# An exponential on VectorE in half octaves: two factors in place of a cubic, in a kernel that shares softmax between ScalarE and VectorE

## The chip, the cores and the metric

The kernel runs on one core of a Trainium2 chip. The metric is device time in microseconds: 894.55 us for the kernel before, the median of three runs (894.08 to 895.09). The profile is of one further execution with a span of 894.9 us. PE is TensorE, DVE VectorE, ACT ScalarE, POOL GpSimd, SP the engine that issues the DMAs.

## What is computed

Two identical layers of a transformer, one after the other, on 2048 tokens of width 448, in bf16:

```python
x = x + A(layernorm(x))     # attention: 16 heads of 28
x = x + B(layernorm(x))     # dense 448 -> 1792 -> 448, squared relu
x = x + A(layernorm(x))
x = x + B(layernorm(x))

# A:  q, k, v = x @ wqkv ; scores = q k^T / sqrt(28)
#     p = softmax(scores) ; o = p @ v ; o @ wo
# B:  h = x @ w1 + b1 ; r = max(h, 0) ; (r * r) @ w2 + b2
```

There is no mask. Each layer has 16 x 2048 x 2048 scores, and each of them goes through an exponential. Nothing is subtracted ahead of it; the sum of the exponentials comes out of the same matmul as the values (a column of ones beside each head's values), and one reciprocal at the end divides.

## The kernel before

**Units and groups.** Attention is cut in units: one head, 128 x 4 keys for one query block of 128, or 128 x 2 keys for a query block of 256, so 512 columns of scores on 128 partitions, one bank of PSUM. `s_stream` (from line 745) takes three units at a time into one score tile of three banks, of which there are two. The matmuls of line 809 fill it. Then line 834, in `e_stream`, exponentiates the tile on ScalarE in one instruction into a bf16 tile `pt`: 1536 columns for three units. Line 982 in `p_stream` multiplies the exponentials with the values into `oT`.

**Units on VectorE.** Where the function `apart` (line 703) allows it, the third bank of a tile holds a unit that ScalarE does not take. ScalarE then exponentiates 1024 columns, and VectorE does the third bank in its own way. The score tile is free for the next matmuls when both have read it (`o.need = 2`, line 789). `apart` looks at what VectorE has been given over the last `SPAN` us of planned time (at most `BUSY`, or `LOW` where the dense layers are behind schedule), at free buffers and at dependencies.

**The exponential on VectorE** (`a_unit` and `a_rest`, lines 880 to 926). The query weights are scaled so that a score is a power of two times 2^FRAC. Line 892 adds a bias, takes a floor and writes the score as int32, so its upper 16 bits are a whole exponent n and its lower 16 bits a fraction f. Line 909 works out a polynomial in f by Horner's rule, in three instructions of the form (h + b) * f. Line 904 writes n times 128 plus a constant as int16, which read as bf16 is 2^n. Line 915 closes: (h + b0) * 2^n, in bf16, into a buffer `pd`. `set_of` (line 869) gives a unit one of two pairs of stores, `v_i` and `v_h` or a part of the key tile that is not in use, and a store `v_e` each for the powers. So one unit is six VectorE instructions.

**What sets the order.** The program's order on every engine is worked out ahead by a list scheduler, the class `Planner`, in Python when the kernel is built. Each piece of work is an `Op` with an engine, a duration that the writer estimated, dependencies and buffers to acquire. A stream is a generator of `Op`s with a priority; the planner takes the candidate that could start first, and by priority among equals. Nothing is reordered at run time. So a changed estimate moves instructions on every engine. The rest of a VectorE unit has a priority that falls as it gets old (the `V_` constants, line 898). Other streams carry the layernorms, the projections and the dense layers (`chain`, from line 1116, with the rectifier of line 1160 and the square of line 1167), the division (`norm_pair`, `norm_stream`), and two that keep TensorE occupied: the score matmuls are written again up to three times (`again`, line 800), and `heat` (line 1203) adds matmuls on a scratch bank.

Of the kernel before, what the change touches and what calls it, by code (L numbers as in the profile page):

```python
# [11 lines left out]
DT = mybir.dt  # L12
AF = mybir.ActivationFunctionType
ALU = mybir.AluOpType
P = 128
# [7 lines left out]

FRAC = 16
EXP_BIAS = -0.207249953 * 2.0 ** FRAC
EXP_LOW = -56.0 * 2.0 ** FRAC
EXP_FIELD = 57.0
EXP_POLY = (73.8872584799254, 51.2040206965149, 17.83949703532682, 3.842974297166197)  # L30
OVER = 0.08
COLD = 7.0
WQD = 1
# [2 lines left out]
DCLK = 0.2  # L36
OWN = 2
HALF = 320
LINES = ((280, 1312, 7.8), (1440, 2040, 7.0))
MARGIN = 2.0  # L40
LOW = 0.6
TURNS = 1
# [13 lines left out]
V_PRIO = 6.0  # L56
V_LATE = 3.6
V_LAST = 1.8
V_AGE = 6
V_PAST = 2  # L60
OWN3 = 0
FIRST = 90
V_FIRST = 9.2
V_WAIT = 5.0
NEAR = 9
FAR = 15
KEEP = 4
# [1 line left out]
LEAD = 20  # L69
LAST = 690  # L70
BUSY = 0.95
SPAN = 12.0
NPT = 11
NOS = 3
AEND = 8
# [142 lines left out]
def kernel(  # L218
# [12 lines left out]
    nc = tc.nc  # L231
# [7 lines left out]

    q_scale = float(DH) ** -0.5 * float(np.log2(np.e)) * 2.0 ** FRAC  # L240

# [5 lines left out]
    const = ctx.enter_context(tc.tile_pool(name="const", bufs=1))  # L247
# [13 lines left out]
    pl = Planner()  # L261
# [164 lines left out]
    e_now = [0, 0]  # L426
# [249 lines left out]
    ends_at = {pi: i for i, (pi, *_) in enumerate(units)}  # L676
# [4 lines left out]
    at = [0]  # L681
# [6 lines left out]
    def behind(i):  # L688

        l = 0 if i < LINES[0][1] else 1  # L690
        a, b, n = LINES[l]
        return done[l] < (min(i, b) - a) / (b - a) * n * per[l] - MARGIN
    pending = [0]

    def sets_of(unit):

        pi, kb, r, hh = unit
        l, qb, *_ = passes[pi]
        if l == 0:
            return R_v if 2 <= qb <= 6 else R_v[:1]  # L700
        return R_v

    def apart(i, now, us, soon=SOON):
# [20 lines left out]
        if any(pl.tok.get(d) is None or pl.tok[d].end + LAT["DVE"] > now for d in needs(units[j])):  # L724
            return None
        if pl.load(SPAN, "DVE") > (LOW if behind(i) else BUSY):
            return None
# [17 lines left out]
    def s_stream():  # L745
        while at[0] < len(units):
# [5 lines left out]
            def fn(e, gi=gi, us=us, js=js):  # L752
# [17 lines left out]
                if j is None:  # L770
                    next_at(js[-1] + 1)
                else:
                    if not own:
                        us, ks = us[:2], ks[:2]
                        gbuf[gi]["n"] = 2
                    us, ks = us + [units[j]], ks + [3]
                    taken.add(j)
                    held[0] += 1
                    pending[0] += 1
                    next_at(at[0])  # L780
                    if own:
                        x = gbuf[gi]["x"] = Op("PE", 0.0, None)
                        x.res = min((r for r in R_m if r.when() is not None), key=lambda r: r.when())
                        x.turn = len(x.res.rel)
                        x.res.rel.append(None)
                        dst.append(bank(x, "mt"))
                    else:
                        x = gbuf[gi]["x"] = o
                        o.need = 2
                    pl.spawn(C_PRIO, a_unit(gi, x, dst[-1], us[-1], passes[us[0][0]][0]))  # L790
# [28 lines left out]
    def apart_from(gi, t):  # L819

        if "read" in gbuf[gi]:
            tc.declare_no_dep(t.ins, gbuf[gi]["read"].ins, reason="both read the scores, in banks of their own")
        gbuf[gi]["read"] = t

    def e_stream():
        gi = 0
        while gi < len(gbuf) or s_left:
# [3 lines left out]
            def fn(e, gi=gi, n=n):  # L831
                e_now[:] = [e_now[0] + n // 512 + ("x" in gbuf[gi]), gi]
                pt = gbuf[gi]["pt"] = ptp.tile([P, 3 * 512], DT.bfloat16, name="pt")
                t = nc.scalar.activation(out=pt[:, 0:n], in_=gbuf[gi]["sc"][:, 0:n], func=AF.Exp,  # L834
                                         scale=float(np.log(2.0)) * 2.0 ** -FRAC)
                if gbuf[gi].get("x") is gbuf[gi]["s"]:
# [8 lines left out]
    def pd_free(unit):  # L845

        pi, kb, r, hh = unit
        l, qb, *_ = passes[pi]
        if l == 0:
            return (R_pd[0], *(R_pd[1:5] if qb <= 6 else R_pd[3:5]))  # L850
        if len(norm_done.get((0, len(blocks[0]) - 1), ())) < G:
            return tuple(R_pd[:1])
        return tuple(R_pd[:1] + R_pd[6:]) if hidden_left[0] else tuple(R_pd[:1] + R_pd[5:])

    def pd_of(o):
        i = R_pd.index(o.res)
        if i == 0:
            return vp.tile([P, 512], DT.bfloat16, name="pd")[:, :]
        if i < 5:
            return V_sb[1][:, 11 + i, :, :].rearrange("p h r -> p (h r)")  # L860
        if i > 5:
            return V_sb[0][:, 8 + i, :, :].rearrange("p h r -> p (h r)")
        return hp.tile([P, QB], DT.bfloat16, name="h")[:, :]

    v_i = const.tile([P, 512], DT.int32, name="v_i")
    v_h = const.tile([P, 512], DT.float32, name="v_h")
    v_e = [const.tile([P, 512], DT.int16, name=f"v_e{i}") for i in range(2)]

    def set_of(res, l):

        k = R_v.index(res)
        two = lambda a: a.rearrange("p (a n) -> p a n", a=2)
        if k == 0:
            i, h = two(v_i[:, :]), two(v_h[:, :])
        else:
            keys = K_sb[1 - l][:, :, S - 512:S] if l == 0 else K_sb[0][:, :, 0:512]
            i, h = keys[:, 0:2, :].bitcast(DT.int32), keys[:, 2:4, :].bitcast(DT.float32)
        return i, h, two(v_e[k][:, :]), two

    def a_unit(gi, x, src, unit, l):  # L880
        yield Op("-", 0.0, None, deps=[("s", gi)])
        b0, b1, b2, b3 = [b * 2.0 ** (FRAC * (4 - k)) for k, b in enumerate(EXP_POLY)]
        box = {}

        def take(e):
            pending[0] -= 1
            box["i"], box["h"], box["e"], two = set_of(c.res, l)
            box["two"] = two
            halves = box["i"].bitcast(DT.uint16).rearrange("p a (n t) -> p a n t", t=2)
            box["f"] = halves[:, :, :, 0]  # L890
            box["n"] = box["i"].bitcast(DT.int16).rearrange("p a (n t) -> p a n t", t=2)[:, :, :, 1]
            t = nc.vector.tensor_scalar(out=box["i"], in0=two(src), scalar1=EXP_BIAS,  # L892
                                        scalar2=EXP_LOW, op0=ALU.add, op1=ALU.max)
            if x is gbuf[gi]["s"]:
                apart_from(gi, t)
        c = Op("DVE", 0.69, take, deps=[("s", gi)], acq=sets_of(unit), rel=x)
        yield c
        pl.spawn(lambda now: V_LAST if e_now[1] - gi >= V_AGE or at[0] > ends_at[unit[0]] + V_PAST else V_LATE if now > c.end + V_WAIT else V_PRIO if gi > FIRST else V_FIRST, a_rest(gi, c, box, unit, (b0, b1, b2, b3)))

    def a_rest(gi, c, box, unit, bs):  # L900
        b0, b1, b2, b3 = bs

        def power(e):
            nc.vector.tensor_scalar(out=box["e"], in0=box["n"], scalar1=128.0, scalar2=128.0 * EXP_FIELD,  # L904
                                    op0=ALU.mult, op1=ALU.add)

        def step(b, begin=False):
            def fn(e):
                nc.vector.scalar_tensor_tensor(out=box["h"], in0=box["f"] if begin else box["h"], scalar=b,  # L909
                                               in1=box["f"], op0=ALU.add, op1=ALU.mult)  # L910
            return fn

        def close(e):
            pd = gbuf[gi]["pd"] = pd_of(o)
            nc.vector.scalar_tensor_tensor(out=box["two"](pd), in0=box["h"], scalar=b0,  # L915
                                           in1=box["e"].bitcast(DT.bfloat16), op0=ALU.add, op1=ALU.mult)
        h = Op("DVE", 0.68, step(b3, True), deps=[c])
        yield h
        p = Op("DVE", 0.42, power, deps=[c])
        yield p  # L920
        for b in (b2, b1):
            h = Op("DVE", 0.68, step(b), deps=[h])
            yield h
        o = Op("DVE", 0.68, close, deps=[h, p], acq=lambda: pd_free(unit), rel=c, sets=("x", gi))
        gbuf[gi]["x"] = o
        yield o

# [341 lines left out]
```

The softmax here doesn't subtract the row's maximum and nothing guards it: scores larger than these inputs give would overflow.

## Time and profile before

| Engine | busy us | share of the span | instructions |
|---|---|---|---|
| TensorE, matmuls | 832.2 | 93% | 12829 |
| VectorE | 794.1 | 89% | 1572 |
| ScalarE | 879.0 | 98% | 707 |
| GpSimd | 38.9 | 4% | 98 |

| Instructions | engine | count | busy us |
|---|---|---|---|
| exponentials, line 834 | ScalarE | 683 (555 of 1536 columns, 128 of 1024) | 864.2 |
| VectorE units: line 892 | VectorE | 127 | 86.9 |
| line 909 | VectorE | 381 | 260.2 |
| line 904 | VectorE | 127 | 53.1 |
| line 915 | VectorE | 127 | 86.6 |
| score matmuls, line 809 | TensorE | 5848 | 325.6 |

The busy time of a group is the sum of what its instructions took; where instructions overlap on their engine, groups add up to more than the engine's own busy time. A share of the span is a mean over stages, so the prediction goes through the stretches of the span and the waits before it names a bound. One of the 128 short groups of ScalarE is the last of all, which has two units only; the other 127 have a unit on VectorE.

### The profile page before, as it was taken

Reading aid. Unit: us, or ns where it says so; the run is one execution under the profiler, and the core shown is the slowest. Engines: PE = TensorE matmul, PEld = TensorE weight load, DVE = VectorE, ACT = ScalarE, POOL = GpSimd, SP = SyncE. Lnnn points to the kernel's source line nnn. Section 1 sums busy time; section 2 is a strip of 40 time slices with the busy share of each in tenths; the row PEclk is TensorE's granted clock in tenths of the full one; section 3 lists DMA queues with packets and bytes.
Section 4 is the critical chain, followed back from the end, with each engine's and each line's share of the span. In section 5 each row is a group of like instructions: output and inputs, shape, how many; then the busy total and the mean of one; then the engine's idle time right before and its main releaser. Section 6 shows DMA issues by size and latency. Waiting matters only on the chain.

```text
span 894.9 us, 29098 instructions
## 1 busy us (share of the span) xinstructions
PE 832.2 (93%) x12829; PEld 458.9 (51%) x12829; DVE 794.1 (89%) x1572; ACT 879.0 (98%) x707; POOL 38.9 (4%) x98
## 2 busy tenths in 40 slices
PE   8999999999999999999989998888999999999998
PEld 4555654554545545454554554444544544545566
DVE  7988999999889999999989999889898999989654
ACT  8999999999999999999999999999999999999995
POOL 3100000000000000100000000001000000000000
PEclk9999999999999999999999999999999999999999
DMA  9100100000000000000000000011000000000100
GB/s 263 37 3 3 27 20 10 14 14 15 14 2 15 14 15 14 13 10 8 2 1 3 2 2 2 3 39 37 13 17 19 20 25 19 20 8 19 32 13 18
DMA packets 33915, 18.43 MB, mean 21 GB/s; under 512 B 18874, under 2 KB 33339, under 8 KB 33788
## 3 DMA queue, kind: packets, MB, share of 16 engines
q1 hardware_dynamic: 33788, 16.58, 6.6%
q8 instruction: 100, 1.64, 0.8%
q14 instruction: 27, 0.22, 0.1%
HBM read 14.26 MB, written 2.07 MB: 18 GB/s over the span
## 4 chain that ended last, share of the span: by engine, by line
ACT 69%; issue 12%; PE 9%; DVE 6%; DMA 2%; SPq 1%; POOL 0%; DVEq 0%; ACTq 0%
ACT pt L834 69%; PE sc L809 3%; PE mt L553 3%; PE oT L982 2%; DVE v_h L909 1%; DMA dn<-oT_sb 1%; DVE K_sb L909 1%; DMA rec<-scr 1%; DVE r L1160 1%; PE sc L553 1%; DVE st L448 1%; DVE oTn L1104 0%; SPq L303 0%; DMA x_sb<-in_A_x_dram 0%; DVE v_e L904 0%
## 5 line engine op out<-in xcount | busy, mean ns | idle before, releaser
L834 ACT ACTIVATE pt<-sc 128x1536 bf16<-128x1536 f32 (+1 forms) x683 | 864.2, 1568 | 3.4 <-PE sc L809 3.1
L809 PE MATMUL sc<-Q_sb,K_sb 32*128 32x256 bf16 (+1 forms) x5848 | 325.6, 266 | 53.5 <-ACT pt L834 47.9
L809 PEld LDWEIGHTS <-K_sb 32*128 32x128 bf16 x5848 | 157.9, 92 | 229.9 <-issue 201.1
L982 PE MATMUL oT<-pt,V_sb 128*32 128x256 bf16 (+1 forms) x4094 | 152.7, 269 | 0.6 <-DVE xnT L505 0.3
L553 PE MATMUL mt<-xnT,w 128*128 128x256 bf16 (+1 forms) x928 | 120.6, 269 | 1.0 <-DVE r L1160 0.7
L982 PEld LDWEIGHTS <-V_sb 128*32 128x32 bf16 x4352 | 92.0, 96 | 47.8 <-issue 44.5
L909 DVE SCALAR_TENSOR_TENSOR K_sb<-K_sb 128x512 f32<-128x512 uint16 x165 | 112.9, 684 | 0.9 <-PE mt L553 0.2
L909 DVE SCALAR_TENSOR_TENSOR v_h<-v_h,v_i 128x512 f32<-128x512 f32 x144 | 98.2, 682 | 0.6
L553 PEld LDWEIGHTS <-w 128*128 128x128 bf16 x952 | 78.5, 98 | 35.7 <-issue 27.4
L1160 DVE TENSOR_SCALAR r<-mt 128x512 bf16<-128x512 f32 x106 | 72.2, 681 | 14.8 <-PE mt L553 14.5
L553 PE MATMUL mt<-w,V_sb 128*128 128x448 bf16 (+2 forms) x288 | 67.6, 345 | 0.0
L892 DVE TENSOR_SCALAR v_i<-sc 128x512 int32<-128x512 f32 x72 | 49.3, 685 | 9.7 <-PE sc L809 9.3
L1113 DVE TENSOR_TENSOR x_sb<-x_sb,mt 128x448 bf16<-128x448 bf16 (+2 forms) x63 | 37.8, 604 | 13.4 <-PE mt L553 13.4
L909 DVE SCALAR_TENSOR_TENSOR v_h<-v_i 128x512 f32<-128x512 uint16 x72 | 49.1, 682 | 0.5
L470 POOL TENSOR_TENSOR ve<-mv,eps_t 128x2 f32<-128x2 f32 (+1 forms) x34 | 8.8, 258 | 842.2 <-DVE mv L449 842.2
L1218 PE MATMUL mt<-xn,ident 128*128 128x448 bf16 x130 | 43.5, 357 | 0.5 <-DVE x_sb L1113 0.3
L892 DVE TENSOR_SCALAR K_sb<-sc 128x512 int32<-128x512 f32 x55 | 37.6, 684 | 5.7 <-PE sc L809 5.5
L448 DVE BATCH_NORM_STATS2 st<-x_sb 128x6 f32<-128x448 bf16 x64 | 39.3, 615 | 1.2 <-DMA x_sb<-in_A_x_dram 1.0
L553 PEld LDWEIGHTS <-V_sb 128*128 128x128 bf16 x302 | 24.8, 98 | 25.5 <-issue 11.2
L915 DVE SCALAR_TENSOR_TENSOR V_sb<-v_h,v_e 128x512 bf16<-128x512 f32 x46 | 31.4, 682 | 0.3
L1167 DVE TENSOR_TENSOR V_sb<-r 128x512 bf16<-128x512 bf16 (+1 forms) x69 | 28.7, 417 | 2.1 <-ACT r L1158 1.5
L904 DVE TENSOR_SCALAR v_e<-v_i 128x512 int16<-128x512 int16 x72 | 30.1, 418 | 0.0
(106 smaller groups left out, 733.6 us busy)
## 6 DMA issues: line engine op xcount, KB each, us to landing
rec<-scr SPq DMA_DIRECT2D x56, 128.0 KB
x_sb<-in_A_x_dram SPq DMA_DIRECT2D x8, 224.0 KB
out_dram<-x_sb SPq DMA_DIRECT2D x15, 112.0 KB
w<-in_B_w_dram SPq DMA_DIRECT2D x1, 1568.0 KB
w<-in_B_w_dram SPq DMA_DIRECT2D x1, 1344.0 KB
dn<-oT_sb SPq DMA_DIRECT2D x56, 4.0 KB
V_sb<-in_A_wqkv_dram SPq DMA_DIRECT2D x4, 168.0 KB
scr<-dn SPq DMA_DIRECT2D x28, 8.0 KB
```

Of the source, the lines that this page charges most:

```text
L448: nc.vector.bn_stats(out=st[:, :], in_=x_sb[:, t0 + j, :])
L553: nc.tensor.matmul(box["t"][:, c0:c0 + n], lhsT=lhsT() if callable(lhsT) else lhsT, rhs=rhs, start=a, stop=b)
L809: nc.tensor.matmul(dst[k][:, i * nt * P:(i + 1) * nt * P], lhsT=K_sb[l][rows, g, (kb + i) * P:(kb + i + 1) * P], rhs=Q_sb[rows, g, t0 * P: ...
L834: t = nc.scalar.activation(out=pt[:, 0:n], in_=gbuf[gi]["sc"][:, 0:n], func=AF.Exp, scale=float(np.log(2.0)) * 2.0 ** -FRAC)
L892: t = nc.vector.tensor_scalar(out=box["i"], in0=two(src), scalar1=EXP_BIAS, scalar2=EXP_LOW, op0=ALU.add, op1=ALU.max)
L904: nc.vector.tensor_scalar(out=box["e"], in0=box["n"], scalar1=128.0, scalar2=128.0 * EXP_FIELD, op0=ALU.mult, op1=ALU.add)
L909: nc.vector.scalar_tensor_tensor(out=box["h"], in0=box["f"] if begin else box["h"], scalar=b, in1=box["f"], op0=ALU.add, op1=ALU.mult)
L915: nc.vector.scalar_tensor_tensor(out=box["two"](pd), in0=box["h"], scalar=b0, in1=box["e"].bitcast(DT.bfloat16), op0=ALU.add, op1=ALU.mult)
L982: nc.tensor.matmul(box["t"][DHP * hh:DHP * hh + DHP, 0:n], lhsT=V_sb[l][:, kb + i, 4 * g + hh, :], rhs=p[:, c0:c0 + n], start=begin and kb ...
L1113: nc.vector.tensor_tensor(out=x_sb[:, tb, lo:hi], in0=x_sb[:, tb, lo:hi], in1=t[:, 0:hi - lo], op=ALU.add)
L1160: nc.vector.tensor_scalar(out=r[:, 0:w], in0=t[:, 0:w], scalar1=0.0, scalar2=None, op0=ALU.max)
L1218: nc.tensor.matmul(t[:, 0:D], lhsT=ident[:, :], rhs=xns[0][:, 0:D], start=True, stop=True)
```

## The change

The exponential on VectorE gets another form. The integer is now in half octaves: `FRAC` is 17, so the upper 16 bits of the int32 count halves of a power of two, and the lower 16 bits are the fraction of a half octave. A float whose bits are n times 2^22 plus a constant has mantissas that take two values in turn, half a unit apart. With an offset of 13573 x 2^7, which is 0.2071 of the mantissa's range, they are 1.2071 and 1.7071, whose ratio is the square root of two, as is that of 2.4142 to 1.7071; so bits that are linear in n give exact half octaves. The new line 904 writes these bits as int32 into `v_e`, a store of 32-bit elements now, and they are read as fp32. A third-degree polynomial in the fraction is split in two factors: the linear one multiplies the power (`first`), the quadratic one is worked out as (f + lin) * f (`square`) and closed with a constant in the last instruction. So one unit is five instructions: line 890 (as 892), 904 (power), 910 (`first`), 916 (`square`), 923 (`close`). In the power's place in the planner the estimate stays at 0.42 us; the chain of estimates loses one of 0.68 us.

Around it, four constants of the planner are changed: the target for the dense layers' progress in the first layer (`LINES`), two that set when a unit's rest gets urgent (`V_AGE`, `V_WAIT`), and the window over which VectorE's load is judged (`SPAN`).

```diff
-FRAC = 16
-EXP_BIAS = -0.207249953 * 2.0 ** FRAC
+FRAC = 17
+EXP_BIAS = -0.19498194355419685 * 2.0 ** FRAC
 EXP_LOW = -56.0 * 2.0 ** FRAC
-EXP_FIELD = 57.0
-EXP_POLY = (73.8872584799254, 51.2040206965149, 17.83949703532682, 3.842974297166197)
+EXP_BASE = 72.0 * 2.0 ** 23 + 13573.0 * 2.0 ** 7
+EXP_POLY = (4.12317870205982 * 2.0 ** 16, 3.06764719893404 * 2.0 ** 16, 29.439149859494734 * 2.0 ** 32)
-LINES = ((280, 1312, 7.8), (1440, 2040, 7.0))
+LINES = ((280, 1312, 8.0), (1440, 2040, 7.0))
-V_AGE = 6
+V_AGE = 7
-V_WAIT = 5.0
+V_WAIT = 4.5
-SPAN = 12.0
+SPAN = 14.0
...
-    v_h = const.tile([P, 512], DT.float32, name="v_h")
-    v_e = [const.tile([P, 512], DT.int16, name=f"v_e{i}") for i in range(2)]
+    v_e = const.tile([P, 512], DT.int32, name="v_e")
...
-            nc.vector.tensor_scalar(out=box["e"], in0=box["n"], scalar1=128.0, scalar2=128.0 * EXP_FIELD,
+            nc.vector.tensor_scalar(out=box["e"], in0=box["n"], scalar1=2.0 ** 22, scalar2=EXP_BASE,
                                     op0=ALU.mult, op1=ALU.add)
-
-        def step(b, begin=False):
-            def fn(e):
-                nc.vector.scalar_tensor_tensor(out=box["h"], in0=box["f"] if begin else box["h"], scalar=b,
-                                               in1=box["f"], op0=ALU.add, op1=ALU.mult)
-            return fn
+        p = Op("DVE", 0.42, power, deps=[c])
+        yield p
+
+        def first(e):
+            nc.vector.scalar_tensor_tensor(out=flt("e"), in0=box["f"], scalar=root, in1=flt("e"),
+                                           op0=ALU.add, op1=ALU.mult)
+        g = Op("DVE", 0.68, first, deps=[p])
+        yield g
+
+        def square(e):
+            nc.vector.scalar_tensor_tensor(out=flt("i"), in0=box["f"], scalar=lin, in1=box["f"],
+                                           op0=ALU.add, op1=ALU.mult)
+        h = Op("DVE", 0.68, square, deps=[c])
+        yield h
 
         def close(e):
             pd = gbuf[gi]["pd"] = pd_of(o)
-            nc.vector.scalar_tensor_tensor(out=box["two"](pd), in0=box["h"], scalar=b0,
-                                           in1=box["e"].bitcast(DT.bfloat16), op0=ALU.add, op1=ALU.mult)
-        h = Op("DVE", 0.68, step(b3, True), deps=[c])
-        yield h
-        p = Op("DVE", 0.42, power, deps=[c])
-        yield p
-        for b in (b2, b1):
-            h = Op("DVE", 0.68, step(b), deps=[h])
-            yield h
-        o = Op("DVE", 0.68, close, deps=[h, p], acq=lambda: pd_free(unit), rel=c, sets=("x", gi))
+            nc.vector.scalar_tensor_tensor(out=box["two"](pd), in0=flt("i"), scalar=low, in1=flt("e"),
+                                           op0=ALU.add, op1=ALU.mult)
+        o = Op("DVE", 0.68, close, deps=[g, h], acq=lambda: pd_free(unit), rel=c, sets=("x", gi))
```

## The prediction

> **What bounds the kernel now.** I read the page's busy times first, then its chain, then the groups with shapes kept apart, then stretches of the span, and last the waits of the three busy engines. Busy shares alone leave three candidates:
>
> ```profile
> PE 832.2 (93%) x12829; PEld 458.9 (51%) x12829; DVE 794.1 (89%) x1572; ACT 879.0 (98%) x707; POOL 38.9 (4%) x98
> ```
>
> The chain names one of them:
>
> ```profile
> ACT 69%; issue 12%; PE 9%; DVE 6%; DMA 2%; SPq 1%; POOL 0%; DVEq 0%; ACTq 0%
> ACT pt L834 69%; PE sc L809 3%; PE mt L553 3%; PE oT L982 2%; DVE v_h L909 1%; DMA dn<-oT_sb 1%; DVE K_sb L909 1%; DMA rec<-scr 1%; DVE r L1160 1%; PE sc L553 1%; DVE st L448 1%; DVE oTn L1104 0%; SPq L303 0%; DMA x_sb<-in_A_x_dram 0%; DVE v_e L904 0%
> ```
>
> It is ScalarE's exponential, line 834. The stretches (engine busy us, instruction count) say that this holds nearly everywhere:
>
> ```profile
> core 0: us, PE busy (x) PEld busy (x) DVE busy (x) ACT busy (x) POOL busy (x), PEclk, DMA share, GB/s
> 100.00:580.00 480.00, 447.99 (x6747) 242.94 (x6748) 444.93 (x858) 479.00 (x382) 18.70 (x48) 1.00 0.04 10
> 580.00:645.00 65.00, 57.11 (x913) 31.76 (x908) 58.59 (x122) 63.85 (x51) 2.75 (x6) 1.00 0.11 28
> 645.00:800.00 155.00, 146.03 (x2160) 75.73 (x2157) 141.60 (x273) 155.00 (x125) 3.02 (x7) 1.00 0.06 19
> 800.00:878.00 78.00, 73.27 (x1547) 44.87 (x1548) 54.34 (x108) 78.00 (x61) 1.63 (x4) 1.00 0.08 22
> ```
>
> ScalarE is idle for 1 us of 480, 1.2 of 65, none of 233; VectorE is idle for 35, 6 and 37 of the same. The waits (total us, times, longest us) say who is late for whom; for VectorE I show its costliest and the two of line 892, which reads the scores. ScalarE:
>
> ```profile
> ACT pt L834 <- PE sc L809: 3.1, 8, 0.7
> ```
>
> and in the other direction
>
> ```profile
> PE sc L809 <- ACT pt L834: 47.9, 130, 0.9
> ```
>
> and VectorE's own:
>
> ```profile
> DVE r L1160 <- PE mt L553: 14.5, 22, 1.9
> DVE v_i L892 <- PE sc L809: 9.3, 10, 1.9
> DVE K_sb L892 <- PE sc L809: 5.5, 7, 2.1
> ```
>
> TensorE waits 47.9 us for ScalarE to free score banks, ScalarE 3.1 us for TensorE; VectorE, where it waits, waits for TensorE. So the span is paced by ScalarE from 20 us to 878 us, and what counts is how many score units ScalarE has to exponentiate. VectorE's 7% of idle time in the middle (35 of 480) is the reserve that lets it take units over.
>
> **Prices.** Groups with shapes kept apart (count | busy us, mean ns of one):
>
> ```profile
> L834 ACT ACTIVATE pt<-sc 128x1536 bf16<-128x1536 f32 x555 | 776.1, 1647 | 2.8 <-PE sc L809 2.5 <-ACT pt L834 0.2
> L834 ACT ACTIVATE pt<-sc 128x1024 bf16<-128x1024 f32 x128 | 147.9, 1225 | 0.6 <-PE sc L809 0.6
> L909 DVE SCALAR_TENSOR_TENSOR v_h<-v_h,v_i 128x512 f32<-128x512 f32 x144 | 98.2, 682 | 0.6
> L1160 DVE TENSOR_SCALAR r<-mt 128x512 bf16<-128x512 f32 x105 | 71.8, 683 | 14.8 <-PE mt L553 14.5
> L892 DVE TENSOR_SCALAR v_i<-sc 128x512 int32<-128x512 f32 x72 | 49.3, 685 | 9.7 <-PE sc L809 9.3
> L904 DVE TENSOR_SCALAR v_e<-v_i 128x512 int16<-128x512 int16 x72 | 30.1, 418 | 0.0
> ```
>
> The reader should see two things. A two-unit group is 1647 - 1225 = 422 ns shorter than a three-unit one. And a 512-wide VectorE instruction costs 0.68 us, except line 904, which costs 0.42. Durations overlap on the engines, so I use the pace. On ScalarE the 683 groups keep it busy for 864.2 us (page, part 5): 555a + 128b = 864.2 with a - b = 0.422 gives a = 1.344 and b = 0.922 us. On VectorE the timeline gives starts:
>
> ```profile
> 310.56 0.69 DVE L892 TENSOR_SCALAR v_i<-sc 128x512 int32<-128x512 f32 x1 [1.63 <-PE sc L809]
> 311.28 0.69 DVE L909 SCALAR_TENSOR_TENSOR v_h<-v_i 128x512 f32<-128x512 uint16 x1
> 311.89 0.68 DVE L892 TENSOR_SCALAR K_sb<-sc 128x512 int32<-128x512 f32 x1
> 312.49 0.42 DVE L904 TENSOR_SCALAR v_e<-v_i 128x512 int16<-128x512 int16 x1
> 312.82 0.69 DVE L909 SCALAR_TENSOR_TENSOR v_h<-v_h,v_i 128x512 f32<-128x512 f32 x1
> ```
>
> A full instruction takes 0.60 us from start to start (311.89 to 312.49), line 904 0.33 us, and an instruction right behind the one whose result it reads 0.12 us more (310.56 to 311.28: 0.72).
>
> **What the Trainium skill says.** "VectorE: DVE Perf Modes", section on the TRN2 errata, gives ScalarE 172 cycles plus one per element at 1.2 GHz for a PSUM source; per 512 elements that is 427 ns, and the trace agrees with 422. The same page, section "The perf-mode tier table", gives `tensor_scalar` twice the rate for fp32 within SBUF (1227 ns for 2048 elements) and a two-tensor operation 1x in fp32; its section "Why PSUM operands drop a tier" leaves 1x to an fp32 PSUM operand. The trace agrees where it has the cases: 0.68 us for the two-tensor line 909 and for lines 892 and 1160, whose source lies in PSUM; 0.42 us for the SBUF-only line 904, although its input has a step of two. No row of before has a 32-bit output at the double rate. "SBUF — State Buffer", section "Who interferes with whom", says that such a double-rate instruction blocks GpSimd while it runs; GpSimd is busy for 38.9 us in all, and line 904 is of that kind already.
>
> **The change part by part.** (1) A unit on VectorE has six instructions before: 892, 909 three times, 904, 915; five after: 890, 904, 910, 916, 923, with one of the cubic's steps gone. Four of the five keep their kind (PSUM to int32; two-tensor with a strided uint16; two-tensor that closes in bf16), so 0.60 us each. (2) The power instruction, new line 904, now writes int32 instead of int16. Between SBUF tiles, with [...] one source, I take the double rate, 0.33 us; the bounds are 0.33 and 0.60 (the row of line 1160). So a unit goes from 5 x 0.60 + 0.33 = 3.33 us to 4 x 0.60 + 0.33 = 2.73, or 3.00 at the dear end. (3) The planner, at 0.68 us less a unit in its own account, gives VectorE more units. The built order of the changed kernel has 150 of them instead of 127, still in 683 ScalarE groups: 532 of three units and 151 of two, instead of 555 and 128. So 23 groups shrink by 0.422 us: 23 x 0.422 = 9.7 us off ScalarE, on the path. (4) VectorE in sum: 127 x 3.33 = 423 us before, 150 x 2.73 = 410 after, 13 less, on an engine that is not the bound. Its other instructions are the same but for one rectifier that moves from ScalarE to it (0.6 us, after the last exponential). (5) TensorE issues 116 fewer score matmuls (5848 to 5732; these are repeats that keep it occupied) and 6 fewer filler matmuls (130 to 124). It has 47.9 us of waiting to give; I cost this at nothing, hidden behind ScalarE. (6) The half-octave constants, the bias and the floor are immediates: nothing. Line 834's scale is one too. The second store v_e goes and v_h becomes v_e; the unit's close (line 923) is still what releases the pair of tiles, and the chain behind it has one step less. (7) The planner's constants (the lines for the dense layers' progress 7.8 to 8.0, ages, the load window of 14 us) cost nothing themselves; they move where units lie. Two-unit groups that follow each other directly go from 30 to 37 times; there are no three in a row.
>
> Sum: 894.55 - 9.7 = 884.9 us, if the opening (to 20 us), the tail (878 to 895 us, whose order is the same but for that rectifier) and the present stalls stay.
>
> No wait is added. The wait that could lengthen is TensorE's for a bank that VectorE must read: the tile of scores is released by ScalarE and by line 890 both, and behind that matmul queue all later scores. With less VectorE work per us it should not.
>
> **Rivals.** *Stalls eat part of it.* ScalarE's path from 9.5 to 879 us holds some jitter and hand-over beyond its pace, and a two-unit group leaves TensorE 0.42 us less to refill. For: more pairs of short groups. Against: 3.1 us of waits now. If each of the 23 new short groups cost a wait of 0.2 us (the mean of the present 8 is 0.4), that is 4.6 us: 889.5.
>
> *VectorE becomes the bound* (the slower side). If the int32 output runs at 1x, VectorE's units cost 150 x 3.00 = 450 us, 27 more than now. From 60 to 800 us it is busy for 681 of 740 us (stretches of 20 to 120 us added up), 59 idle, mostly waiting for TensorE. About nine tenths of the 27, 24 us, fall there: 705 of the 731 us that ScalarE would need. If its waits fell to 26 us nothing would be lost; if they stayed at 59 the stretch would last 764, 33 more. Half way is 17 more: 885 + 17 = 902, slower. For: no row of before shows this form. Against: the price in the skill, and line 904's rate despite its strided read.
>
> *TensorE becomes the bound and the time stays.* It is busy for 93%, but a busy matmul engine is not one at its peak, as the skill's opening page "Trainium Kernel Development and Optimization" (section "Performance Expectations") warns too, and it waits 47.9 us for ScalarE here. It would have to lose all that: 894.5.
>
> **How the numbers follow.** Clean gain, 882 to 888 us: 0.65. Part eaten, 888 to 892.8: 0.20. No change, within 0.2% (892.8 to 896.3): 0.05. VectorE-bound or otherwise slower, around 902: 0.10. The likeliest gives 884.9. The range takes the first two cases with a little for a better hand-over than now, 881.5 to 893; the 0.33 us bound lies in it, the dear 0.60 us bound mostly beyond it, which is in the 2 in 10 left out.
>
> **What would show it.** ScalarE: 532 and 151 groups, 854.5 us busy on line 834, still idle by under 1% between 100 and 800 us, the last exponential ending near 869. VectorE: line 904 at 0.42 us with an int32 output, lines 910, 916, 923 at 0.68; busy about 781 us. TensorE still waiting over 35 us for ScalarE. I am wrong if line 904 shows 0.68 us, if ScalarE's waits for line 809 rise past 10 us, or if the hand-over between the two attention layers, 580 to 645 us, or the tail grows by several us.

## The result, and the profile after

The changed kernel takes 885.99 us (median of 6, 885.07 to 888.95), and the kernel before, run beside it, 895.45 us. The ratio is 0.990, 95% interval 0.988 to 0.992. The prediction was 884.9 us, with a range of 881.5 to 893. The profiled execution has a span of 884.1 us against 894.9.

Busy times and chain of the page, after:

```profile
PE 824.2 (93%) x12707; PEld 453.5 (51%) x12707; DVE 786.8 (89%) x1561; ACT 868.4 (98%) x706; POOL 39.1 (4%) x98
...
ACT 71%; PE 11%; issue 11%; DVE 4%; DMA 2%; SPq 1%; POOL 0%; DVEq 0%; ACTq 0%
```

ScalarE is busy for 10.6 us less and its share is what it was. VectorE falls by 7.3 us only. The stretches of after (the last exponential starts 11 us earlier than in before, so the last two stretches end earlier too):

```profile
100.00:580.00 480.00, 447.56 (x6719) 239.36 (x6719) 440.76 (x853) 479.50 (x387) 18.30 (x48) 1.00 0.04 10
580.00:645.00 65.00, 59.12 (x940) 32.09 (x940) 59.63 (x121) 64.35 (x53) 2.12 (x4) 1.00 0.12 33
645.00:790.00 145.00, 137.36 (x2004) 72.70 (x2003) 136.99 (x265) 145.00 (x118) 3.34 (x6) 1.00 0.06 18
790.00:868.00 78.00, 72.91 (x1573) 45.09 (x1570) 55.49 (x112) 77.94 (x61) 2.51 (x6) 1.00 0.07 19
```

ScalarE is idle for 0.5 us of 480, 0.65 of 65 and next to nothing after that, as little as before, but does 387 instructions where it did 382 in the first stretch. The groups that changed, shapes kept apart:

```profile
L834 ACT ACTIVATE pt<-sc 128x1536 bf16<-128x1536 f32 x532 | 750.5, 1658 | 1.8 <-PE sc L809 1.8
L834 ACT ACTIVATE pt<-sc 128x1024 bf16<-128x1024 f32 x151 | 174.9, 1236 | 0.9 <-PE sc L809 0.9
L916 DVE SCALAR_TENSOR_TENSOR v_i<-v_i 128x512 f32<-128x512 uint16 x85 | 58.3, 686 | 1.5
L910 DVE SCALAR_TENSOR_TENSOR v_e<-v_i,v_e 128x512 f32<-128x512 uint16 x85 | 58.2, 685 | 0.8
L904 DVE TENSOR_SCALAR v_e<-v_i 128x512 int32<-128x512 int16 x85 | 35.6, 418 | 0.3
```

532 and 151 groups, 422 ns apart (1658 - 1236). The power instruction with its int32 output takes 418 ns, as the one with int16 output did. The waits of ScalarE and TensorE for each other:

```profile
ACT pt L834 <- PE sc L809: 2.6, 6, 0.8
```

and

```profile
PE sc L809 <- ACT pt L834: 41.8, 116, 0.7
```

ScalarE still hardly waits, and TensorE waits for it by 6 us less.

**One sum for every kernel.** From the starts of line 834 in a trace the span can be cut in four: the first exponential's start; the pace, which is 1.330 us after each three-unit group and 0.904 us after each two-unit group (the medians of both traces; the last group is left out); what ScalarE loses over that pace up to the last group's start; and the tail from there to the end. The four add up by construction, and the pace follows from the two counts alone, so the table says where a kernel's time is, not why. "Hand-over" is the part of the loss that falls between 540 and 660 us, where attention passes from the first layer to the second.

| kernel | groups of 3, 2 | first | pace | loss | of it hand-over | tail | span |
|---|---|---|---|---|---|---|---|
| before | 555, 128 | 9.5 | 853.0 | 15.0 | 3.1 | 17.5 | 894.9 |
| after | 532, 151 | 9.4 | 843.2 | 13.9 | 2.0 | 17.7 | 884.1 |
| same plan, new arithmetic | 555, 128 | 10.0 | 853.0 | 13.1 | 2.0 | 17.5 | 893.5 |
| after, load limit 0.88 | 544, 139 | 9.8 | 848.3 | 13.1 | 1.5 | 17.9 | 889.0 |
| after, load window 12 | 538, 145 | 9.4 | 845.7 | 12.6 | 1.7 | 17.7 | 885.3 |
| after, old constants | 532, 151 | 9.7 | 843.2 | 18.0 | 6.6 | 25.1 | 896.0 |
| before, new constants | 557, 126 | 9.7 | 853.8 | 13.8 | 1.5 | 24.9 | 902.2 |
| old constants, second target 7.3 | 534, 149 | 9.7 | 844.0 | 17.3 | 5.2 | 17.6 | 888.6 |
| new constants, second target 7.3 | 560, 123 | 9.6 | 855.1 | 14.4 | 1.5 | 17.7 | 896.7 |
| old constants, first target 7.9 | 533, 150 | 9.5 | 843.6 | 13.2 | 1.5 | 17.7 | 884.0 |
| slow power | 532, 151 | 9.4 | 843.2 | 34.9 | 6.7 | 17.7 | 905.2 |
| own store | 529, 154 | 9.7 | 841.9 | 15.6 | 3.6 | 19.2 | 886.4 |
| more units | 529, 154 | 9.7 | 841.9 | 15.6 | 5.6 | 19.1 | 886.4 |

Of the 10.8 us between the two spans, 9.8 are pace (23 groups), 1.1 loss, and the tail gives 0.2 back. The 1.1 us need not come from the change: the execution of before that was profiled took 896.67 us, 1.2 more than the 895.45, its granted TensorE clock was 0.91 between 200 and 220 us, and 1.5 us of its loss fall just there, at 213 to 217 us. The third row has before's order and a loss of 13.1.

### The profile page after: what moved, and what is told of

Its sections match the earlier page's. It is cut to its first block, busy times and chain, and to the rows that moved or that the text cites. A ratio compares the mean times of both kernels' runs of the same rounds, so it can differ in the third digit from the quotient of the medians.

```text
span 884.1 us, 28887 instructions
## 1 busy us (share of the span) xinstructions
PE 824.2 (93%) x12707; PEld 453.5 (51%) x12707; DVE 786.8 (89%) x1561; ACT 868.4 (98%) x706; POOL 39.1 (4%) x98
## 4 chain that ended last, share of the span: by engine, by line
ACT 71%; PE 11%; issue 11%; DVE 4%; DMA 2%; SPq 1%; POOL 0%; DVEq 0%; ACTq 0%
ACT pt L834 71%; PE mt L553 4%; PE sc L809 3%; PE oT L983 2%; DMA dn<-oT_sb 1%; PE sc L553 1%; DMA scr<-dn 1%; DVE st L448 1%; DMA rec<-scr 0%; SPq L303 0%; DMA x_sb<-in_A_x_dram 0%; PE mt L1219 0%; DVE V_sb L923 0%; DVE r L1161 0%; DVE v_i L890 0%
## 5 line engine op out<-in xcount | busy, mean ns | idle before, releaser
L834 ACT ACTIVATE pt<-sc 128x1536 bf16<-128x1536 f32 (+1 forms) x683 | 854.2, 1565 | 2.6 <-PE sc L809 2.6
L809 PE MATMUL sc<-Q_sb,K_sb 32*128 32x256 bf16 (+1 forms) x5732 | 320.3, 265 | 47.8 <-ACT pt L834 41.8
L809 PEld LDWEIGHTS <-K_sb 32*128 32x128 bf16 x5732 | 152.4, 92 | 226.2 <-issue 194.3
L1161 DVE TENSOR_SCALAR r<-mt 128x512 bf16<-128x512 f32 (+1 forms) x107 | 72.7, 680 | 11.2 <-PE mt L553 10.8
L890 DVE TENSOR_SCALAR v_i<-sc 128x512 int32<-128x512 f32 x85 | 58.1, 684 | 4.1 <-PE sc L809 3.4
L916 DVE SCALAR_TENSOR_TENSOR v_i<-v_i 128x512 f32<-128x512 uint16 x85 | 58.3, 686 | 1.5
L910 DVE SCALAR_TENSOR_TENSOR v_e<-v_i,v_e 128x512 f32<-128x512 uint16 x85 | 58.2, 685 | 0.8
L890 DVE TENSOR_SCALAR K_sb<-sc 128x512 int32<-128x512 f32 x65 | 44.4, 684 | 13.4 <-PE sc L809 13.3
L916 DVE SCALAR_TENSOR_TENSOR K_sb<-K_sb 128x512 f32<-128x512 uint16 x65 | 44.5, 685 | 1.3 <-PE mt L553 0.2
L910 DVE SCALAR_TENSOR_TENSOR K_sb<-K_sb 128x512 f32<-128x512 uint16 x65 | 44.4, 684 | 1.0 <-PE mt L553 0.7
L553 PEld LDWEIGHTS <-V_sb 128*128 128x128 bf16 x302 | 24.9, 98 | 25.1 <-issue 11.2
L923 DVE SCALAR_TENSOR_TENSOR V_sb<-v_i,v_e 128x512 bf16<-128x512 f32 x54 | 36.8, 682 | 0.2
L904 DVE TENSOR_SCALAR v_e<-v_i 128x512 int32<-128x512 int16 x85 | 35.6, 418 | 0.3
```

The lines of the kernel that those rows point to most:

```text
L553: nc.tensor.matmul(box["t"][:, c0:c0 + n], lhsT=lhsT() if callable(lhsT) else lhsT, rhs=rhs, start=a, stop=b)
L809: nc.tensor.matmul(dst[k][:, i * nt * P:(i + 1) * nt * P], lhsT=K_sb[l][rows, g, (kb + i) * P:(kb + i + 1) * P], rhs=Q_sb[rows, g, t0 * P: ...
L910: nc.vector.scalar_tensor_tensor(out=flt("e"), in0=box["f"], scalar=root, in1=flt("e"), op0=ALU.add, op1=ALU.mult)
L916: nc.vector.scalar_tensor_tensor(out=flt("i"), in0=box["f"], scalar=lin, in1=box["f"], op0=ALU.add, op1=ALU.mult)
L923: nc.vector.scalar_tensor_tensor(out=box["two"](pd), in0=flt("i"), scalar=low, in1=flt("e"), op0=ALU.add, op1=ALU.mult)
L1161: nc.vector.tensor_scalar(out=r[:, 0:w], in0=t[:, 0:w], scalar1=0.0, scalar2=None, op0=ALU.max)
```

## The experiments

The theory at the start was that of the prediction: ScalarE paces, so the gain is the number of groups that shrink. Rival one: VectorE paces too, so cheaper units are worth time by themselves. Rival two: the planner's constants carry the gain.

### The arithmetic without the extra units

The five instructions are put in the plan of before. The planner is told of six, the extra one being empty, so every other engine gets its order of before.

```diff
+        q = Op("DVE", 0.68, None, deps=[c])     # counted, nothing issued
+        yield q
         p = Op("DVE", 0.42, power, deps=[c])
...
 # the links between the estimates as before
-        g = Op("DVE", 0.68, first, deps=[p])
+        g = Op("DVE", 0.68, first, deps=[q])
-        h = Op("DVE", 0.68, square, deps=[c])
+        h = Op("DVE", 0.68, square, deps=[g])
-        o = Op("DVE", 0.68, close, deps=[g, h], ...)
+        o = Op("DVE", 0.68, close, deps=[h, p], ...)
...
-LINES, V_AGE, V_WAIT, SPAN of the changed kernel
+LINES, V_AGE, V_WAIT, SPAN of the kernel before
```

> The new five-instruction exponential in the order of before: old planner constants, and the planner still counts six instructions a unit, the fourth of 0.68 us being empty. So 127 units on VectorE and 555 + 128 ScalarE groups, in the same order on every engine. Theory (ScalarE paces, the gain is the number of short groups): no gain, 894 to 897 us, with VectorE's busy time down by about 127 x 0.60 = 76 us. Rival one (VectorE paces too, a cheaper unit is worth time by itself): 890 us or less. Rival two (the constants move the work to better places): no gain either.

895.96 us, ratio 1.000 (0.999 to 1.002). Its busy times:

```profile
PE 830.9 (93%) x12829; PEld 458.4 (51%) x12829; DVE 736.7 (82%) x1445; ACT 878.9 (98%) x707; POOL 39.3 (4%) x98
```

VectorE has 127 instructions fewer and 57.4 us less busy time than before, and the time is the same. (76 us were expected. The durations added up fall by 85 us, but 28 us of overlap between neighbours go with them, since the instructions left behind stand apart more often.) VectorE's work as such is worth nothing here. Rival one falls for the kernel before: what counts is what the freed time is used for.

### The planner's constants apart from the arithmetic

```diff
 # "old constants": the changed kernel with
-LINES = ((280, 1312, 8.0), ...)   V_AGE = 7   V_WAIT = 4.5   SPAN = 14.0
+LINES = ((280, 1312, 7.8), ...)   V_AGE = 6   V_WAIT = 5.0   SPAN = 12.0
 # "new constants": the kernel before with the reverse
```

> The changed kernel with the four planner constants as before; the planner still finds 150 units for VectorE, 532 + 151 groups. Theory: the whole gain, 885 to 888 us. Rival two (the constants carry the gain): 891 us or more.

> The kernel before with only the four planner constants changed: six instructions a unit, 125 units, 557 + 126 groups. Theory: two groups longer than before, 2 x 0.42 = 0.8 us more, 895 to 898 us. Rival two: 891 us or less.

Both expectations failed. With the old constants the changed arithmetic takes 897.83 us (ratio 1.003, 1.002 to 1.004) with the very same 532 and 151 groups; with the new constants the old arithmetic takes 905.07 us (1.010, 1.008 to 1.012). The first result lies where rival two had put it. So the count of groups does not settle the time alone. But the constants are no gain by themselves: on the old arithmetic they cost 9.5 us. ScalarE's timeline at the end shows the larger part (in brackets the idle time before an instruction, and what ended it). After, where the first line's run of exponentials ends at 868:

```profile
862.42 5.53 ACT L834 ACTIVATE pt<-sc 128x1536 bf16<-128x1536 f32 x4
869.78 0.60 ACT L1159 ACTIVATE r<-mt 128x512 bf16<-128x512 f32 x1 [1.84 <-PE mt L553]
```

and the changed kernel with the old constants:

```profile
862.95 9.35 ACT L834 ACTIVATE pt<-sc 128x1536 bf16<-128x1536 f32 x7
880.72 0.60 ACT L1159 ACTIVATE r<-mt 128x512 bf16<-128x512 f32 x1 [8.42 <-PE mt L553]
```

With the old constants ScalarE is done at 872 and then waits 8.4 us for a matmul of the dense layer: its last blocks come later. The stores of the output say the same. The second layer's tokens are stored in seven blocks of 256 and two of 128. The last store of the seventh block is issued 5.2 us ahead of the start of the last exponential in the changed kernel, and 2.9 us behind it with the old constants. The tail is 25.1 us for 17.7. Most of the rest is in the hand-over, 6.6 us lost for 2.0; with the new constants on the old arithmetic the hand-over loses only 1.5, and the tail of 24.9 us makes the whole difference to before.

### The tail alone

The built order shows the tail ahead of a run. What tells is how many matmuls of line 553 (nearly all of them of the dense layers) stand behind the last score matmul. It is 161 before and after, and 168 in both slow versions. The traces show which seven are more: three with w2, and four of the attention's output projection, that of the eighth block, which the shorter order has done by then. (The first expectation below counts 31 and 28 with w2, without 14 that write to a score bank in either order.) One number of the planner, the target for the dense layers' progress in the second layer, puts it back to 161 in both.

```diff
 # on "old constants" and on "new constants"
-LINES = (..., (1440, 2040, 7.0))
+LINES = (..., (1440, 2040, 7.3))
```

> The changed kernel with the old planner constants (which took 897.8 us) and the second layer's progress target at 7.3 for 7.0. In the built order the matmuls of the dense layers that stand behind the last score matmul fall from 168 to 161, of which those with w2 from 31 to 28, as in the changed kernel; 534 + 149 groups, so two are wider (0.8 us more). Theory (the long tail, 25.1 us after the last exponential's start for 17.7, took 7.4 us of the gain, and stalls between the two attention layers some 4 to 8 more): 897.8 - 7.4 + 0.8 = 891 us, and the tail 17.5 to 18 us. Rival (the loss lies in stalls all over, or in VectorE's lateness): 895 us or more.

> The kernel before with the new planner constants (which took 905.1 us) and the second layer's progress target at 7.3 for 7.0: 560 + 123 groups for 557 + 126, three wider, 1.3 us more; 161 dense matmuls behind the last score matmul for 168. Theory: 905.1 - 7.4 + 1.3 = 899 us, and the tail 17.5 to 18 us. Rival: 904 us or more.

892.07 us (ratio 0.997) and 898.39 us (1.004), each within 1.1 us of what was expected, with tails of 17.6 and 17.7 us. So the tail, 7.4 and 7.2 us, is shown as a term of its own, in either arithmetic. Not all of it need be the order: in the long tails the granted TensorE clock is 0.93, in the short ones 0.98 to 1.00. The versions with more units, below, have the short order at 0.91 and a tail that is 1.4 us longer, so an estimate from these is that about 1 us of the 7 is the clock. Whether the order brings the lower clock with it is open. In the first of the two versions the hand-over still loses 5.2 us.

A further version has three of the old constants, and 7.9 as the first layer's target, half way between old and new.

```diff
-LINES = ((280, 1312, 8.0), ...)   V_AGE = 7   V_WAIT = 4.5   SPAN = 14.0
+LINES = ((280, 1312, 7.9), ...)   V_AGE = 6   V_WAIT = 5.0   SPAN = 12.0
```

> The changed kernel with three of the four planner constants as before and the first layer's progress target at 7.9, between the old 7.8 and the new 8.0. 533 + 150 groups, one wider than in the changed kernel, and 161 dense matmuls behind the last score matmul. Theory (what counts is the number of groups, the tail and the hand-over that the order happens to give, not the constants as such): tail 17.6 us, 886.4 us if the hand-over from 540 to 660 us goes as in the changed kernel, 889.5 us if it loses as much as with the target at 7.8. Rival (the new constants are what makes the gain): 892 us or more.

885.96 us (0.990, 0.988 to 0.991), the changed kernel's time with almost none of its constants: tail 17.7, hand-over loss 1.5. Rival two falls as it was put. The constants act only through the order that the planner makes of them, and an order is good if the tail and the hand-over come out short in it. Why the hand-over lost 5 to 7 us in two of these orders was not isolated. In that of the old constants TensorE's waits there name VectorE's additions of partial attention sums (line 1008, 4.2 us in three waits between 540 and 660 us), which stand behind units on VectorE; that is read, not tested.

### The worth of a unit

Two versions of the changed kernel with fewer units and a good tail.

```diff
 # half_units
-BUSY = 0.95
+BUSY = 0.88
 # span_12
-SPAN = 14.0
+SPAN = 12.0
```

> The changed kernel with the planner's limit on VectorE's load at 0.88 for 0.95: 138 units, 544 + 139 groups, so 12 of the 23 groups are three units wide again. Theory: 12 x 0.422 = 5.1 us more than the changed kernel, about 891 us. Rival one (VectorE is a bound in the changed kernel): less load on VectorE, so 886 us or less.

> The changed kernel with the load window alone back at 12 us: 538 + 145 groups, 161 dense matmuls behind the last score matmul. Theory: 6 groups wider, 6 x 0.42 = 2.5 us more than the changed kernel, 888.5 us. Rival (the count of short groups does not matter): 886 us.

891.02 us and 887.50 us: 5.0 us more than the changed kernel for 12 groups, and 1.5 us for 6. The first is the pace's 12 x 0.426 = 5.1 us. The second is 1.0 us under what was expected: its pace is 2.5 us longer, as its counts make it, but its trace loses 1.3 us less. So the slope holds with the tail and the hand-over kept, to about 1 us.

### If the power instruction had been slow

The disputed cost of the prediction, made to happen: the power as a two-tensor instruction that takes its constant from a tile filled once at the start, in the changed kernel's order (names shortened).

```diff
-nc.vector.tensor_scalar(out=e, in0=n, scalar1=2.0 ** 22, scalar2=EXP_BASE, op0=ALU.mult, op1=ALU.add)
+nc.vector.scalar_tensor_tensor(out=e, in0=n, scalar=2.0 ** 22, in1=base, op0=ALU.mult, op1=ALU.add)
```

> The changed kernel, in its order, with the power instruction as a two-tensor operation (its constant comes from a tile) and so at about 0.68 us for 0.42; the planner still counts 0.42. VectorE has 150 x 0.27 = 40 us more of durations to issue. Prediction's rival: VectorE becomes the bound, about 902 us. Theory after the result (VectorE still waits some 80 us for others, so it takes part of the load in its waits): 887 to 895 us, with ScalarE waiting for score matmuls that wait for line 890.

907.49 us, 1.014 (1.013 to 1.016). The instruction, from the groups of its trace:

```profile
L906 DVE SCALAR_TENSOR_TENSOR v_e<-v_i,base 128x512 int32<-128x512 int16 x85 | 58.1, 683 | 0.3
```

and ScalarE's and TensorE's waits in it:

```profile
ACT pt L834 <- PE sc L809: 13.9, 32, 1.6
...
PE sc L809 <- ACT pt L834: 27.9, 82, 0.6
PE mt L553 <- DVE r L1163: 5.2, 12, 1.0
PE sc L809 <- DVE v_i L892: 4.4, 9, 0.8
PE mt L553 <- DVE xnT L505: 3.5, 7, 1.2
PE mt L553 <- DVE x_sb L1116: 3.2, 4, 1.1
```

Each unit costs VectorE 0.27 us more and the kernel is 21.5 us longer than the changed one. TensorE now waits for VectorE at many places, the reading of scores (line 892 here) among them, and ScalarE waits 13.9 us for score matmuls where it waited 2.6. So the changed kernel, in this order, stands close to the edge at which VectorE becomes the bound: of 150 x 0.265 = 40 us more in durations, over half came out at the end, and the milder theory written after the result was wrong. The order is the one laid out for 0.42 us; what the planner makes of 0.68 us was not tried. Together with the first experiment this says that VectorE's time is free in one direction only, downwards.

### More units

The timeline of after shows a cost that the prediction had not counted. Line 910 reads the fraction in the unit's integers; line 916, right behind it, writes its own result over them:

```profile
316.99 0.69 DVE L910 SCALAR_TENSOR_TENSOR K_sb<-K_sb 128x512 f32<-128x512 uint16 x1 [0.68 <-PE mt L553]
317.72 0.69 DVE L916 SCALAR_TENSOR_TENSOR K_sb<-K_sb 128x512 f32<-128x512 uint16 x1
...
319.53 0.42 DVE L904 TENSOR_SCALAR v_e<-v_i 128x512 int32<-128x512 int16 x1
319.98 0.69 DVE L910 SCALAR_TENSOR_TENSOR v_e<-v_i,v_e 128x512 f32<-128x512 uint16 x1
```

0.73 us from start to start, not 0.60, although 916 uses no result of 910; and 0.45 us from the power to its reader, not 0.33. A version gives the quadratic factor a store of its own in one of the two sets and puts it between the power and the linear factor. With other planner constants it has 153 units.

```diff
+    v_h = const.tile([P, 512], DT.float32, name="v_h")
...
-            nc.vector.scalar_tensor_tensor(out=flt("i"), in0=box["f"], scalar=lin, in1=box["f"], ...)
+            nc.vector.scalar_tensor_tensor(out=box["h"], in0=box["f"], scalar=lin, in1=box["f"], ...)
 # order in that set: power, square, first, close
-BUSY = 0.95   LOW = 0.6   SPAN = 14.0   first target 8.0
+BUSY = 0.97   LOW = 0.8   SPAN = 12.0   first target 7.8
```

> The changed kernel with a store of its own for the quadratic factor in one of the two sets (so that it need not wait for the reader of the fraction it would overwrite) and placed between the power and the linear factor there; load limit 0.97, lower limit 0.8, window 12 us, progress target 7.8. 153 units on VectorE: 529 + 154 groups for 532 + 151, and 161 dense matmuls behind the last score matmul as in the changed kernel. Theory: 3 x 0.42 = 1.3 us less than the changed kernel, 884 to 885.5 us, and fewer starts 0.72 us apart on VectorE. Rival (VectorE or the hand-over is at its limit): 887 us or more.

886.66 us (0.991, 0.989 to 0.992): no gain over the changed kernel. The timeline of this version shows both cases side by side, the own store and the store in place:

```profile
306.20 0.68 DVE L918 SCALAR_TENSOR_TENSOR v_h<-v_i 128x512 f32<-128x512 uint16 x1
306.80 0.68 DVE L911 SCALAR_TENSOR_TENSOR v_e<-v_i,v_e 128x512 f32<-128x512 uint16 x1
...
308.33 0.68 DVE L911 SCALAR_TENSOR_TENSOR K_sb<-K_sb 128x512 f32<-128x512 uint16 x1
309.05 0.69 DVE L918 SCALAR_TENSOR_TENSOR K_sb<-K_sb 128x512 f32<-128x512 uint16 x1
```

0.60 us for the pair that shares reads only (median of 46 such pairs in the trace), 0.72 for the pair in which the second overwrites what the first read (median of 40). The two sets differ in their tiles too, but that is not the reason: in the changed kernel, with both sets in place, 43 pairs in `v_i` and `v_e` and 30 in the key tile start 0.72 us apart alike. Starts that came 0.08 to 0.14 us late behind an instruction of 0.68 or 0.42 us fell from 175 in the changed kernel, 21 us in all, to 125 and 15 us in this version, and no time was gained by it. A last version takes 153 units by the planner's constants alone.

```diff
-BUSY = 0.95   LOW = 0.6   V_AGE = 7   V_WAIT = 4.5   second target 7.0
+BUSY = 1.05   LOW = 0.8   V_AGE = 8   V_WAIT = 5.0   second target 7.2
```

> The changed kernel with other planner constants (load limit 1.05, lower limit 0.8, ages 8 and 5.0, second target 7.2): 153 units on VectorE, 529 + 154 groups, 161 dense matmuls behind the last score matmul. Theory: 3 x 0.42 = 1.3 us less than the changed kernel, 884.7 us, if no stall is added. Rival (VectorE is at its limit with 150 units): 886 us or more, with more than 14 us over ScalarE's pace.

887.79 us (0.992, 0.990 to 0.993): again no gain. In both traces the pace is 1.3 us shorter, as three groups should make it. The hand-over loses 1.6 and 3.6 us more than in the changed kernel, and the tail is 1.4 to 1.5 us longer. The tail in the second of them, and in the changed kernel:

```profile
867.00:886.40 19.40, 16.27 (x203) 12.25 (x201) 8.26 (x19) 6.88 (x11) 0.75 (x2) 0.91 0.05 14
866.00:884.10 18.10, 14.99 (x209) 11.59 (x203) 8.26 (x19) 7.08 (x11) 0.75 (x2) 0.98 0.05 15
```

VectorE is busy for 8.26 us in both, TensorE for 16.27 us against 14.99, and the granted TensorE clock is 0.91 against 0.98. The first of the two versions has 0.91 there too; all nine other traces with the same 161 matmuls behind the last score matmul have 0.98 to 1.00 and tails of 17.5 to 17.9 us. So the longer tail goes with the clock, and one profile of each is too few to lay it on the version. Both profiles are of executions at a mean clock of 0.996, that of the first version of its slowest. At a clock of 1.0 the first version has one run, of 885.46 us, just within what was expected of it but also within the changed kernel's four, 885.07 to 886.10; the second has one of 887.19. No version was found that beats the changed kernel clear of noise.

## Why the prediction was right

**The bound and its price held.** 23 groups shrank by 0.422 us, 9.7 us; line 834's busy time fell from 864.2 to 854.2, the pace by 9.8, the median by 9.5. The fewer-units versions give the same slope from the other side. The result lies in the likeliest of the forecast's cases.

**The power instruction held** at the cheap end: 419 ns at the median in both stores, 359 to 428 over all 150. The Trainium skill's table ("VectorE: DVE Perf Modes", section "The perf-mode tier table") gives `tensor_scalar` in fp32 within SBUF twice the rate of a two-tensor operation. It has no row for a 16-bit input at a step of two with a 32-bit output, and the prediction carried the fp32 row over to it; the traces agree, with 418 ns against 683 as a two-tensor instruction, 0.33 us against 0.60 from start to start. The slow version shows what hung on it: the rival's 902 us would have been 907.

**One term was mis-sized: VectorE's sum.** 13 us less were predicted, 7.3 were measured. The durations of VectorE's instructions, added up, did fall by 13.7 us, from 894.1 to 880.4, but what they overlap fell too, from 100.0 to 93.6. The step "Four of the five keep their kind (...), so 0.60 us each" left out who stands behind whom, although the prediction had read the 0.12 us more behind a result off the timeline. In before, the planner's order put the power between the first two steps of the cubic, so that the 0.12 us was often hidden. In after, the power's reader follows it, and the in-place square follows the reader of what it overwrites. The starts that came 0.08 to 0.14 us late went from 105, 12.5 us in all, to 175, 21 us. Of each 0.12 us, 0.08 shows as busy time: an instruction of 0.68 us overlaps the next by 0.08 where the two start 0.60 us apart, and not at all at 0.72. That VectorE is not the bound hid the error.

**One step was right by its check in one place, by luck in another.** "The planner's constants (...) cost nothing themselves; they move where units lie" is true of the value 885.99 only because the built order of the changed kernel keeps both the tail and the hand-over. For the tail the prediction had looked at that order. For the hand-over it assumed that the present stalls stay, and that held by luck: 2.0 us lost for 3.1. Where units lie was worth up to 7.4 us in the tail and 4.6 in the hand-over. The prediction names both places among the signs of being wrong, but sizes them only as "several us" and makes no rival of them; its rival of eaten stalls took its size from the present mean wait per group. With the same arithmetic, the same number of groups and the old constants the forecast would have been wrong by 13 us.

**The other rivals.** The new short groups brought no stalls: ScalarE waits 2.6 us for scores, 3.1 before. TensorE did not become the bound: it waits 41.8 us for ScalarE, as forecast (over 35). VectorE would have become it at 0.60 us for the power; half way between all and nothing, 17 us, was a little too mild for what came to 21.5.

## What to carry to other kernels

When a helper engine shares the bounding engine's work, price the change in units moved times what one unit saves on the bound, and treat cheaper work on the helper as worth nothing until it is used. Where a scheduler lays out the whole order, a change of costs throws the order anew: count in the built order what stands behind the last piece of the bounding work, since that tail, and the passage between stages, can take back the whole gain. Where an engine runs its instructions in the order of the program, look at who overwrites what the instruction ahead of it reads: a buffer saved can cost 0.12 us a time. That is worth mending only where this engine sets the time; here it bought nothing.

## What was not expected of the hardware

In these traces a VectorE instruction that overwrites what the one directly ahead of it reads starts 0.72 us after it, not 0.60, although it needs none of its results (40 pairs against 46 in one trace, 73 pairs in the changed kernel). Each of the 73 carries a wait for a semaphore that VectorE's own instructions raise, so this is the price of that wait; what the chip does without it was not tried. The short duration of the power needs neither a unit step nor equal widths: int16 at a step of two to int32 took 418 ns for 512 elements, 683 as a two-tensor instruction.
